# First rows of a Fourier and token-mixing kernel in a hand-made order, with imaginary products woven in and small tiles declared first

## The chip, the cores and the metric

The kernel runs on one core of a Trainium2 chip. Its engines each work through a queue of their own and wait for each other by semaphores: PE (TensorE) multiplies matrices, ACT (ScalarE) and DVE (VectorE) work element by element, POOL (GpSimd) and SP (SyncE) mostly issue transfers. The metric is the device time of one execution in microseconds (us). Before the change it is 887.15 us, the median of three runs from 886.62 to 887.22.

## The reference

`x` has 2048 rows (tokens) of 640 values in float32. Each row is normalized to `xn`. The output is the sum of `x`, a two-dimensional Fourier transform of `xn` of which the real part is kept, and a two-layer network across the token axis.

```python
x = A_x
xn = _layernorm(x, axis=-1)
# _A_ref: a = xn @ dft_hid_re.T, b = xn @ dft_hid_im.T, y = dft_seq_re @ a - dft_seq_im @ b
# _B_ref: u = gelu(xn^T @ w1 + b1), y = (u @ w2 + b2)^T
return x + _A_ref(xn, A_dft_seq_re, A_dft_seq_im, A_dft_hid_re, A_dft_hid_im) + _B_ref(xn, B_w1, B_b1, B_w2, B_b2)
```

## The kernel before, in words

**Precision.** Every float32 operand of a product is split into a high part (`high`, a copy on ACT that rounds to the product's format, L111) and a low part (`low`, a subtraction on DVE, L114). A product of two operands is three matmuls (`three`, L122 to L124): high by high, high by low, low by high. Each loads its own weights: 128 rows by 128 columns of the normalized `x`, while 512 columns of a Fourier matrix move through.

**Steps.** The work is a list of steps. A step cuts one loaded piece of a matrix of 128 x 512 (its *top* is the high part on ACT, its *bottom* the low part on DVE; three places `cut0` to `cut2` are taken in turn) and multiplies it. `turn_of(i)` issues, in this order: the loads planned for turn i, the reads of finished banks, the work on rows, the top of step i + 2, extras, background jobs, the bottom of step i + 2, and the matmuls of step i.

**The first columns.** The first 16 steps (`BLOCK`) work with the first eight groups of 128 rows. Step i has m = i // 8 (real or imaginary Fourier matrix) and k = i % 8 (group of rows), and five products (15 matmuls), one per 128 channels of `x`, each into a PSUM bank of its own. The banks of the real half are read after step 7 (L434), those of the imaginary half after step 15, and both are stored by POOL. Ahead of group k's first product, the group of rows has to be loaded, its mean and variance found (`moments`, DVE, L166 and L167), a square root taken (`root`, DVE L173 and ACT L174), the two factors worked out by four or five small DVE instructions (`inverse` and `offset`, L180 to L189), the rows normalized in place (`normalize`, ACT, L213), and split into high (ACT, two copies of 512 and 128 columns) and low (DVE).

**Order.** Turns up to 7 are issued outside the block with a manual schedule, so a scheduler orders their instructions on each engine. From turn 8 on the order is that of the program. SP issues the loads of rows (L414) and pieces (L415), and waits where a place is still in use; ACT, DVE and PE work strictly through their own queues.

**Warming up.** While the first loads are under way PE multiplies a tile of zeros (`idle`) 20 times (L108).

**Second part.** After the first columns come seven groups of 32 steps each (`columns`), 216 matmuls of 512 columns in a group. They work with sums of rows that background jobs make: the first three groups with those of the lower half of the rows, the last four with those of the upper half. The weights lie in eight operand places `slab0` to `slab7` of 17,920 bytes per partition; place `slab7` serves the last four groups' every fourth row, `n13`. Behind them come three more stages with matmuls of 320 columns.

**Places.** Tiles of the pool `keep` lie one behind another in the order in which their tags are first declared. Before the change that is: `b1_sb`, `b2_sb`, `one`, then `slab7` (by the tile `idle`), then the three small tiles `mv`, `norm` and `again` of 128 bytes per partition each, then `slab4`, `slab5`, `slab0` to `slab3` and the rest.

Of the kernel before, what the change touches and what calls it, by code (L numbers as in the profile page):

```python
# [8 lines left out]
F32 = mybir.dt.float32  # L9
R32 = mybir.dt.float32r  # L10
BF16 = mybir.dt.bfloat16
AF = mybir.ActivationFunctionType
# [28 lines left out]

# [13 lines left out]
def fnet_plus_mixer(  # L55
# [45 lines left out]
    one = keep.tile([P, 1], F32, name="one")  # L101
# [8 lines left out]
    def high(hi, src):  # L110
        nc.scalar.activation(hi, src, AF.Copy)  # L111

    def low(lo, src, hi):
        nc.vector.tensor_sub(lo, src, hi.bitcast(F32))  # L114
# [4 lines left out]
    def three(psum, w, m, first, last):  # L119

        (wh, wl), (mh, ml) = w, m
        nc.tensor.matmul(psum, wh, mh, start=first, stop=False, skip_group_check=True)  # L122
        nc.tensor.matmul(psum, wh, ml, start=False, stop=False, skip_group_check=True)  # L123
        nc.tensor.matmul(psum, wl, mh, start=False, stop=last, skip_group_check=True)  # L124
# [63 lines left out]
    def offset(to, ks):  # L188
        nc.vector.scalar_tensor_tensor(to[:, 1, ks], mv[:, ks, 0], -1.0, to[:, 0, ks], op0=ALU.mult, op1=ALU.mult)  # L189

    def factors(ks):
        inverse(norm[:, 0, ks], *root(mv[:, ks, 1]))
        offset(norm, ks)
# [15 lines left out]

        return [rooted, inverted]  # L210

    def normalize(k, row, by):
        nc.scalar.activation(row, row, AF.Identity, scale=by[:, 0, k : k + 1], bias=by[:, 1, k : k + 1])  # L213


    def pair_at(tag):
# [27 lines left out]
    def fifth(a, which, i):  # L244
        return a[:, which, 7 * Q + i * P : 7 * Q + (i + 1) * P]
# [4 lines left out]
    def sums_of_rows(h, q, row, lower, apart=False):  # L250
# [37 lines left out]
        return [job1, job2, job3, job4] + [job5] * apart + [job6]  # L288


    x_slab = [
        keep.tile([P, 7, D], F32, name="x0", tag="slab4"), keep.tile([P, 1, D], F32, name="x1", tag="slab5"),
    ]
    x_in = [x_slab[k // 7][:, k % 7, :] for k in range(8)]
    for q in range(4):
        place_fixed(0, q)

    def first_rows(k):

        normalize(k, x_in[k], norm)  # L300
# [31 lines left out]
    def later_moments(q):  # L332

        def get():
            for i in range(2):
                nc.sync.dma_start(later_pair(q)[:, i, :], x_rows[8 + q + 4 * i])

        loads[6 + 2 * q].append(get)
        for i in range(2):
            extras[8 + 2 * q + i].append(lambda i=i: moments(8 + q + 4 * i, later_pair(q)[:, i, :]))  # L340

    def later_factors():

# [49 lines left out]
    def c_tile():  # L393

        i = c_turn[0] = (c_turn[0] + 1) % 6
        return c_place[i // 3][:, i % 3, :]

    def store_y(h, m, c, j, t):
        if h == 0:
            nc.gpsimd.dma_start(y_part[m][c][:, j, :], t)  # L400
        else:
            nc.gpsimd.dma_start(y_part[m][c][:, j, :], t, accum_op=ALU.add)

    def first_columns():

        raw = pieces[1].rearrange("p a q c -> p (a q) c")
        banks = {}
        for i in range(BLOCK):
            m, k = i // 8, i % 8

            def load(m=m, k=k, i=i):
                if m == 0:
                    for r in ROWS_AT.get(k, ()):
                        nc.sync.dma_start(x_in[r], x_rows[r])  # L414
                nc.sync.dma_start(raw[:, i % 8, :], dft_seq[m * NC, k])  # L415

            def rows(m=m, k=k):
                if m == 0:
                    first_rows(k)
                    for k0, k1 in GROUPS_AT.get(k, ()):  # L420
                        for r in range(k0, k1):
                            moments(r, x_in[r])
                        factors(slice(k0, k1))

            def products(w, m=m, k=k):
                for j in range(ND):
                    if k == 0:
                        banks[j] = psum[(5 * m + j) % 8]
                    three(banks[j], channels(k, j), w, k == 0, k == 7)

            def read(m=m):
                for j in range(ND):
                    c = c_tile()
                    nc.scalar.activation(c, banks[j], AF.Copy)  # L434
                    store_y(0, m, 0, j, c)

            loads[i - LOADS].append(load)
            sums[i - AHEAD].append(rows)
            steps.append(cut_piece(lambda i=i: raw[:, i % 8, :], CH) + (products,))
            if k == 7:  # L440
                reads[i + 1].append(read)
        loads[-LOADS].append(lambda: None)

    def columns(g, h, c):

# [363 lines left out]
        )  # L809


    first_columns()
    first_sums = [sums_of_rows(0, q, lambda q=q: x_in[q], lambda q=q: x_in[q + 4], True) for q in range(4)]
    for q in range(4):
        later_moments(q)
# [41 lines left out]
    for t in range(NS // 2):  # L857
        down(1, t, ("ca", "cb")[t % 2])

    ready = {}  # L860

    def do_jobs(n, short=False):

        while n > 0 and jobs and not (short and isinstance(jobs[0], tuple)):
# [24 lines left out]
            steps[i][2](ready.pop(i))  # L889


    by_hand = 8
# [58 lines left out]
```

## Time and profile before

| | us |
|---|---|
| time, median of three runs | 887.15 |
| the profiled execution's own time | 887.16 |
| its span, first to last instruction | 884.9 |
| PE busy | 877.2 |
| DVE busy | 701.8 |
| ACT busy | 525.5 |
| POOL busy | 123.2 |

The span is what the profile sees of the program; 2.26 us of the execution lie around it. The profile's page lists busy time by engine and by line; the views used below are the waits (who waited for whom, with the total, the number of times and the longest) and the timeline (start and length of each instruction, with the idle time before it in brackets and what ended it). A matmul's length in the timeline is not its cost: matmuls overlap, and the cost of one is the distance between two starts.

### The profile page before, as it was taken

Reading aid. Unit: us, or ns where it says so; the run is one execution under the profiler, and the core shown is the slowest. Engines: PE = TensorE matmul, PEld = TensorE weight load, DVE = VectorE, ACT = ScalarE, POOL = GpSimd, SP = SyncE. Lnnn points to the kernel's source line nnn. Section 1 sums busy time; section 2 is a strip of 40 time slices with the busy share of each in tenths; the row PEclk is TensorE's granted clock in tenths of the full one; section 3 lists DMA queues with packets and bytes.
Section 4 is the critical chain, followed back from the end, with each engine's and each line's share of the span. In section 5 each row is a group of like instructions: output and inputs, shape, how many; then the busy total and the mean of one; then the engine's idle time right before and its main releaser. Section 6 shows DMA issues by size and latency. Waiting matters only on the chain.

```text
span 884.9 us, 14021 instructions
## 1 busy us (share of the span) xinstructions
PE 877.2 (99%) x4964; PEld 798.8 (90%) x4964; DVE 701.8 (79%) x1181; ACT 525.5 (59%) x953; POOL 123.2 (14%) x166
## 2 busy tenths in 40 slices
PE   8999999999999999999999999999999999999998
PEld 5888888888888888888999999999999999999998
DVE  8577888796787978787877887998678968986776
ACT  6546576664565566557565555675477766655553
POOL 0101000101121111222010101000122211111111
PEclk9999999999999999999999999999999999999999
DMA  8941463719475555869766766553478797756875
GB/s 292 319 144 66 151 253 102 268 48 329 87 206 89 154 136 114 225 83 184 180 124 156 163 142 193 159 180 133 131 170 182 174 253 183 164 129 133 156 173 124
DMA packets 85542, 147.15 MB, mean 166 GB/s; under 512 B 8416, under 2 KB 35296, under 8 KB 85216
## 3 DMA queue, kind: packets, MB, share of 16 engines
q1 hardware_dynamic: 64848, 95.72, 33.3%
q0 software_dynamic: 20624, 50.54, 30.0%
q8 instruction: 39, 0.64, 0.3%
q14 instruction: 31, 0.25, 0.1%
HBM read 99.63 MB, written 51.84 MB: 171 GB/s over the span
## 4 chain that ended last, share of the span: by engine, by line
PE 96%; DVE 2%; ACT 1%; DMA 1%; issue 0%; SPq 0%
PE psum L124 32%; PE psum L123 32%; PE psum L122 32%; DMA pieces<-in_dft_seq 1%; DVE piece L114 0%; DVE st L166 0%; ACT x L213 0%; DVE n L114 0%; DVE shid L114 0%; ACT piece L111 0%; DVE pair L117 0%; DVE pieces L662 0%; DVE pieces L117 0%; SPq L414 0%; ACT shid L111 0%
## 5 line engine op out<-in xcount | busy, mean ns | idle before, releaser
L114 DVE TENSOR_TENSOR piece<-pieces,piece 128x512 fp32r<-128x512 f32 (+2 forms) x506 | 346.6, 688 | 147.7 <-ACT piece L111 144.3
L111 ACT ACTIVATE piece<-pieces 128x512 fp32r<-128x512 f32 (+2 forms) x506 | 317.9, 629 | 235.1 <-PE psum L124 161.0
L122 PE MATMUL psum<-piece,n 128*128 128x512 f32 x584 | 228.4, 391 | 2.5 <-ACT n L111 2.5
L123 PE MATMUL psum<-piece,n 128*128 128x512 f32 x584 | 228.3, 391 | 0.0
L124 PE MATMUL psum<-piece,n 128*128 128x512 f32 x584 | 227.4, 391 | 0.0
L122 PEld LDWEIGHTS psum<-piece,n 128*128 128x128 f32 x584 | 109.6, 188 | 27.2 <-ACT n L111 3.8
L123 PEld LDWEIGHTS psum<-piece,n 128*128 128x128 f32 x584 | 109.7, 188 | 25.6 <-DVE piece L114 2.0
L124 PEld LDWEIGHTS psum<-piece,n 128*128 128x128 f32 x584 | 109.7, 188 | 23.1
L124 PE MATMUL psum<-sup,piece 128*128 128x320 f32 x392 | 121.5, 310 | 0.0
L124 PE MATMUL psum<-sdown,piece 128*128 128x320 f32 x392 | 121.1, 309 | 0.0
L123 PE MATMUL psum<-sdown,piece 128*128 128x320 f32 x392 | 121.0, 309 | 0.0
L123 PE MATMUL psum<-sup,piece 128*128 128x320 f32 x392 | 121.0, 309 | 0.0
L122 PE MATMUL psum<-sup,piece 128*128 128x320 f32 x392 | 121.0, 309 | 0.0
L122 PE MATMUL psum<-sdown,piece 128*128 128x320 f32 x392 | 121.0, 309 | 0.0
L117 DVE TENSOR_TENSOR pieces<-pieces 128x512 f32<-128x512 f32 (+3 forms) x142 | 112.5, 793 | 2.6
L124 PE MATMUL psum<-shid,piece 128*128 128x320 f32 x280 | 86.9, 310 | 0.1
L123 PE MATMUL psum<-shid,piece 128*128 128x320 f32 x280 | 86.5, 309 | 0.0
L122 PE MATMUL psum<-shid,piece 128*128 128x320 f32 x280 | 86.5, 309 | 0.0
L712 ACT ACTIVATE pair<-psum 128x320 f32<-128x320 f32 x104 | 45.3, 436 | 60.1 <-PE psum L124 59.6
L124 PEld LDWEIGHTS psum<-sup,piece 128*128 128x128 f32 x392 | 73.6, 188 | 0.3
L122 PEld LDWEIGHTS psum<-sup,piece 128*128 128x128 f32 x392 | 73.6, 188 | 0.0
L123 PEld LDWEIGHTS psum<-sup,piece 128*128 128x128 f32 x392 | 73.6, 188 | 0.0
(95 smaller groups left out, 1007.8 us busy)
## 6 DMA issues: line engine op xcount, KB each, us to landing
pieces<-in_dft_seq SPq DMA_DIRECT2D x128, 256.0 KB, 5.6
pieces<-in_w SPq DMA_DIRECT2D x88, 256.0 KB, 3.8
y<-c POOLq DMA_DIRECT2D x84, 256.0 KB, 6.0
out<-pair POOLq DMA_DIRECT2D x38, 320.0 KB, 5.2
pieces<-y SPq DMA_DIRECT2D x32, 320.0 KB, 3.7
pieces<-in_w SPq DMA_DIRECT2D x32, 192.0 KB, 3.1
out<-in_x SPq DMA_DIRECT2D x16, 320.0 KB, 5.9
up<-pair POOLq DMA_DIRECT2D x8, 640.0 KB, 3.3
```

Source lines behind the costliest of these rows:

```text
L111: nc.scalar.activation(hi, src, AF.Copy)
L114: nc.vector.tensor_sub(lo, src, hi.bitcast(F32))
L117: nc.vector.tensor_sub(to, a, b)
L122: nc.tensor.matmul(psum, wh, mh, start=first, stop=False, skip_group_check=True)
L123: nc.tensor.matmul(psum, wh, ml, start=False, stop=False, skip_group_check=True)
L124: nc.tensor.matmul(psum, wl, mh, start=False, stop=last, skip_group_check=True)
L712: nc.scalar.activation(c, b, AF.Copy)
```

## The change

It concerns the first columns, and the order of declarations.

- **Woven steps.** There are 18 steps in place of 16. The first two groups of rows are multiplied by the real piece (15 matmuls) and, right behind it, by the imaginary piece for three of the five channel groups (9 matmuls). The two remaining products of these groups in the imaginary half come last, as two steps of 6 matmuls. The number of matmuls and of loaded pieces is the same; two pieces are cut twice.
- **Order within a step.** A step runs all its high by high matmuls first, then all high by low, then all low by high.
- **Order by hand.** The first eight turns are replaced by a list of words, `START`: `x` and `b` load rows and a piece, `T`, `B` and `P` are a step's top, bottom and matmuls, `M` moments, `R` root, `F` factors, `H` the high part of a group of rows, `N` its normalization in place, `L` its low part. The high part is now normalized straight from the loaded rows (with the first group in pieces of 256, 256 and 128 columns), ahead of the normalization in place.
- **First load.** The first group of rows is loaded as two halves, one of which ACT issues as its first instruction.
- **Sums a step later.** The background jobs begin at turn 10 in place of 8, and the last jobs of each group take the order 2, 3, 0, 1. Moments of two of the later rows move into the list.
- **Bank reads.** The real banks are read at turn 10, three of the imaginary ones at turn 16 and two at turn 18.
- **Warming up.** 13 idle matmuls in place of 20.
- **Places.** `mv`, `norm`, `again` are declared right behind `one`, and the tile of the first rows ahead of `idle`: behind the small tiles now come `slab4`, `slab5`, `slab7`, `slab0` and so on.

```diff
-WARM = 20
-ROWS_AT = {0: (0,), 1: (1,), 2: (2, 3), 3: (4, 5), 4: (6, 7)}
-GROUPS_AT = {0: ((1, 2), (2, 4)), 1: ((4, 6),), 3: ((6, 8),)}
-BLOCK = 16
+WARM = 13
+BLOCK = 18
+FIRST = (
+    [(0, 0, 0, 5), (1, 0, 0, 3), (0, 1, 0, 5), (1, 1, 0, 3)] + [(0, k, 0, 5) for k in range(2, 8)]
+    + [(1, k, 0, 5) for k in range(2, 8)] + [(1, 0, 3, 5), (1, 1, 3, 5)]
+)
+FIRST_AT = [0, 6, 1, 7, 2, 3, 4, 5, 0, 1, 2, 3, 4, 5, 0, 1, 6, 7]
+START = """
+    x0 b0 x1 b1 b2 x2 b3 x3 b4 x4 x5 b5 x6 x7 b6 b7
+    T0 M0 R0 F0 H0 B0 N0 M1 R1 T1 L0 F1 H1 B1 P0
+    M2 T2 N1 B2 L1 b8 P1 M3 T3 R2-3 F2-3 H2 B3 P2
+    M4 T4 N2 B4 L2 b9 P3 M5 H3 T5 R4-5 N3 B5 F4-5 L3 b10 e0 P4
+    M6 H4 T6 N4 B6 L4 b11 P5 H5 M7 R6-7 T7 N5 B7 F6-7 L5 b12 e1 P6
+    H6 T8 M8 N6 B8 L6 b13 P7 H7 T9 M12 N7 B9 L7
+"""
...
+    one = keep.tile([P, 1], F32, name="one")
+    mv = keep.tile([P, NS, 2], F32, name="mv")
+    norm = keep.tile([P, 2, NS], F32, name="norm")
+    again = keep.tile([P, 2, NS], F32, name="again")
...
+    x_slab = [
+        keep.tile([P, 7, D], F32, name="x0", tag="slab4"), keep.tile([P, 1, D], F32, name="x1", tag="slab5"),
+    ]
+    x_in = [x_slab[k // 7][:, k % 7, :] for k in range(8)]
+    nc.scalar.dma_start(x_in[0][:, H2:], x_rows[0][:, H2:])
...
-    mv = keep.tile([P, NS, 2], F32, name="mv")
-    norm = keep.tile([P, 2, NS], F32, name="norm")
-    again = keep.tile([P, 2, NS], F32, name="again")
...
-    def normalize(k, row, by):
-        nc.scalar.activation(row, row, AF.Identity, scale=by[:, 0, k : k + 1], bias=by[:, 1, k : k + 1])
+    def normalize(k, row, by, to=None):
+        nc.scalar.activation(
+            row if to is None else to, row, AF.Identity, scale=by[:, 0, k : k + 1], bias=by[:, 1, k : k + 1]
+        )
...
-        high(two(0), src)
-        high(fifth(a, 0, k // 4), x_in[k][:, 2 * Q :])
-        low(two(1), src, two(0))
-        low(fifth(a, 1, k // 4), x_in[k][:, 2 * Q :], fifth(a, 0, k // 4))
+        whole = [(two, src), (lambda which: fifth(a, which, k // 4), x_in[k][:, 2 * Q :])]
+        if which == 0 and k == 0:
+            whole[:1] = [(lambda which, b=b: two(which)[:, b, :], src[:, b, :]) for b in range(2)]
+        for to, t in whole:
+            if which == 0:
+                normalize(k, t, norm, to(0))
+            else:
+                low(to(1), t, to(0))
...
+            for n, (rows, cols) in enumerate(((0, 0), (0, 1), (1, 0))):
+                for j in range(j0, j1):
+                    begin, end = (2, 1) if m == 1 and j >= 3 else (0, 7)
+                    if n == 0 and k == begin:
+                        banks[m, j] = psum[(5 * m + j) % 8]
+                    nc.tensor.matmul(
+                        banks[m, j], channels(k, j)[rows], w[cols], start=n == 0 and k == begin,
+                        stop=n == 2 and k == end, skip_group_check=True,
+                    )
...
+        reads[10].append(lambda: read(0, range(ND)))
+        reads[16].append(lambda: read(1, range(3)))
+        reads[18].append(lambda: read(1, range(3, ND)))
...
-    timed[8].append(lambda: jobs.extend(j for part in (slice(4), slice(4, 6)) for js in first_sums for j in js[part]))
+    timed[10].append(lambda: jobs.extend(
+        [j for js in first_sums for j in js[:4]] + [j for q in (2, 3, 0, 1) for j in first_sums[q][4:]]
+    ))
...
-    for i in range(-LOADS, by_hand):
-        if i == -AHEAD:
-            moments(0, x_in[0])
-            factors(slice(0, 1))
-        turn_of(i, 0)
     with tc.manual_schedule():
-        for i in range(by_hand, len(steps) + 1):
+        for word in START.split():
+            start[word[0]](*map(int, word[1:].split("-")))
+        for i in range(8, len(steps) + 1):
```

More of the change, by code (lines that the diff above doesn't have):

```diff
@@ L94, in fnet_plus_mixer @@
     b2_sb = keep.tile([P, NS], F32, name="b2_sb")
+    one = keep.tile([P, 1], F32, name="one")
+    mv = keep.tile([P, NS, 2], F32, name="mv")
+    norm = keep.tile([P, 2, NS], F32, name="norm")
+    again = keep.tile([P, 2, NS], F32, name="again")
     out_rows = [out[t * P : (t + 1) * P, :] for t in range(NS)]
     x_rows = [x[t * P : (t + 1) * P, :] for t in range(NS)]
+    x_slab = [
[3 more added lines that the diff above has]
+    nc.scalar.dma_start(x_in[0][:, H2:], x_rows[0][:, H2:])
     part_up = [dram.tile([P, 2, D], F32, name=f"up{r}") for r in range(NF2)]
     y_part = [[dram.tile([P, ND, CH], F32, name=f"y{m}{c}") for c in range(NC)] for m in range(2)]
-    one = keep.tile([P, 1], F32, name="one")
     nc.vector.memset(one, 1.0)
@@ L288, in sums_of_rows, with first_rows @@
         return [job1, job2, job3, job4] + [job5] * apart + [job6]
[L291 to L294, printed above, removed]
     for q in range(4):
         place_fixed(0, q)
-    def first_rows(k):
-        normalize(k, x_in[k], norm)
+    def first_rows(k, which):
         a = fixed[0][k % 4]
@@ L330, in later_pair, with later_load, later_moments @@
         return later[0][:, q] if q < 3 else later[1]
[L332 to L338, printed above, removed]
+    def later_load(q):
         for i in range(2):
-            extras[8 + 2 * q + i].append(lambda i=i: moments(8 + q + 4 * i, later_pair(q)[:, i, :]))
+            nc.sync.dma_start(later_pair(q)[:, i, :], x_rows[8 + q + 4 * i])
+    def later_moments(k):
+        moments(k, later_pair(k % 4)[:, (k - 8) // 4, :])
     def later_factors():
@@ L407, in first_columns @@
         banks = {}
[L408 to L441, printed above, removed]
@@ L442, in first_columns, with load, products @@
-        loads[-LOADS].append(lambda: None)
+        vq = {}
+        def load(i):
+            m, k = FIRST[i][:2]
+            nc.sync.dma_start(raw[:, FIRST_AT[i], :], dft_seq[m * NC, k])
+        def products(w, m, k, j0, j1):
+            for n, (rows, cols) in enumerate(((0, 0), (0, 1), (1, 0))):
[7 more added lines that the diff above has]
+                    )
@@ new lines, in read @@
+        def read(m, js):
+            for j in js:
+                c = c_tile()
+                nc.scalar.activation(c, banks[m, j], AF.Copy)
+                store_y(0, m, 0, j, c)
+        for i, (m, k, j0, j1) in enumerate(FIRST):
+            steps.append(
+                cut_piece(lambda i=i: raw[:, FIRST_AT[i], :], CH)
+                + (lambda w, at=(m, k, j0, j1): products(w, *at),)
+            )
+        reads[10].append(lambda: read(0, range(ND)))
+        reads[16].append(lambda: read(1, range(3)))
@@ new lines, in first_columns, with row, top, bottom @@
+        reads[18].append(lambda: read(1, range(3, ND)))
+        for i in range(14, 16):
+            loads[i - 6].append(lambda i=i: load(i))
+        def row(k):
+            if k == 0:
+                nc.sync.dma_start(x_in[0][:, :H2], x_rows[0][:, :H2])
+            else:
+                nc.sync.dma_start(x_in[k], x_rows[k])
+        def top(i):
+            steps[i][0]()
+        def bottom(i):
+            ready[i] = steps[i][1]()
+        def run(i):
+            steps[i][2](ready.pop(i))
@@ new lines, in rooted, with factored @@
+        def rooted(k, to=None):
+            ks = slice(k, (to or k) + 1)
+            vq[k] = root(mv[:, ks, 1])
+        def factored(k, to=None):
+            ks = slice(k, (to or k) + 1)
+            inverse(norm[:, 0, ks], *vq[k])
+            offset(norm, ks)
+        return {
+            "x": row, "b": load, "e": later_load, "T": top, "B": bottom, "P": run,
+            "M": lambda k: moments(k, x_in[k]) if k < 8 else later_moments(k), "R": rooted, "F": factored,
+            "H": lambda k: first_rows(k, 0), "N": lambda k: normalize(k, x_in[k], norm),
+            "L": lambda k: first_rows(k, 1),
+        }
@@ L809, in down @@
         )
-    first_columns()
+    ready = {}
+    start = first_columns()
     first_sums = [sums_of_rows(0, q, lambda q=q: x_in[q], lambda q=q: x_in[q + 4], True) for q in range(4)]
-    for q in range(4):
-        later_moments(q)
-    timed[8].append(lambda: jobs.extend(j for part in (slice(4), slice(4, 6)) for js in first_sums for j in js[part]))
+    for q in range(2, 4):
+        loads[4 + 2 * q].append(lambda q=q: later_load(q))
+    for i, k in enumerate((9, 13, 10, 14, 11, 15)):
+        extras[8 + i].append(lambda k=k: later_moments(k))
+    timed[10].append(lambda: jobs.extend(
+        [j for js in first_sums for j in js[:4]] + [j for q in (2, 3, 0, 1) for j in first_sums[q][4:]]
+    ))
     for g in range(2 * NC - 1):
@@ L858, in fnet_plus_mixer @@
         down(1, t, ("ca", "cb")[t % 2])
-    ready = {}
     def do_jobs(n, short=False):
@@ L889, in turn_of @@
             steps[i][2](ready.pop(i))
-    by_hand = 8
-    for i in range(-LOADS, by_hand):
-        if i == -AHEAD:
-            moments(0, x_in[0])
-            factors(slice(0, 1))
-        turn_of(i, 0)
     with tc.manual_schedule():
-        for i in range(by_hand, len(steps) + 1):
+        for word in START.split():
+            start[word[0]](*map(int, word[1:].split("-")))
+        for i in range(8, len(steps) + 1):
             n_jobs, short = (1, i < BLOCK), False
```

## The prediction

> **What bounds the kernel now.** I read the page first, then PE's waits, then the timeline of the first 30 us on PE, ACT and DVE, then PE's timeline again in the last four groups.
>
> ```profile
> span 884.9 us, 14021 instructions
> PE 877.2 (99%) x4964; PEld 798.8 (90%) x4964; DVE 701.8 (79%) x1181; ACT 525.5 (59%) x953; POOL 123.2 (14%) x166
> ```
>
> PE is the bound. Where does it still stand idle? Its waits over the whole run are two rows:
>
> ```profile
> PE psum L122 <- ACT n L111: 2.5, 3, 1.5
> PE psum L108 <- DVE idle L105: 1.2, 1, 1.2
> ```
>
> All three waits on `n`, the rows' high parts, lie ahead of the first three steps:
>
> ```profile
> 1.23 6.65 PE L108 MATMUL psum<-idle 128*128 128x512 bf16 x20 [1.23 <-DVE idle L105]
> 9.42 0.50 PE L122 MATMUL psum<-piece,n 128*128 128x512 f32 x1 [1.54 <-ACT n L111]
> 13.44 0.50 PE L122 MATMUL psum<-piece,n 128*128 128x512 f32 x1 [0.30 <-ACT n L111]
> 17.80 0.50 PE L122 MATMUL psum<-piece,n 128*128 128x512 f32 x1 [0.65 <-ACT n L111]
> 21.34 0.39 PE L122 MATMUL psum<-piece,n 128*128 128x512 f32 x1
> 24.74 0.39 PE L122 MATMUL psum<-piece,n 128*128 128x512 f32 x1
> ```
>
> From 21.34 on a step of 15 matmuls takes 24.74 - 21.34 = 3.40, so 0.2267 each. By 21.34 there were 45, worth 10.20: the products stand as if they had run without a gap from 11.14. I call this the virtual start. Whatever moves it moves the end, since PE shows no wait afterwards. Why is the first product as late as 9.42?
>
> ```profile
> 4.43 0.63 ACT L111 ACTIVATE piece<-pieces 128x512 fp32r<-128x512 f32 x1 [2.19 <-DMA pieces<-in_dft_seq]
> 5.17 0.20 ACT L174 ACTIVATE q<-v 128x1 f32<-128x1 f32 x1
> 7.19 0.63 ACT L111 ACTIVATE piece<-pieces 128x512 fp32r<-128x512 f32 x1 [1.82 <-DMA pieces<-in_dft_seq]
> 7.73 0.91 ACT L213 ACTIVATE x<-x,norm 128x640 f32<-128x640 f32 x1
> 8.75 0.81 ACT L111 ACTIVATE n<-x 128x512 fp32r<-128x512 f32 x2
> ...
> 5.71 0.15 DVE L180 RECIPROCAL r<-q 128x1 f32<-128x1 f32 x1
> 7.15 0.10 DVE L189 SCALAR_TENSOR_TENSOR norm<-mv,norm 128x1 f32<-128x1 f32 x1
> ```
>
> The root is done at 5.37, but the factors only at 7.25, with the next rows' moments in between on DVE; ACT stands behind a second piece that lands at 7.19, then normalizes 640 columns, then copies.
>
> The last four groups, whose waits are too short for the list, hide a second loss. Starts of steps of nine matmuls, first in an early group, then in a late one:
>
> ```profile
> 71.66 0.39 PE L122 MATMUL psum<-piece,n 128*128 128x512 f32 x1
> 73.70 0.39 PE L122 MATMUL psum<-piece,n 128*128 128x512 f32 x1
> ...
> 217.68 0.39 PE L122 MATMUL psum<-piece,n 128*128 128x512 f32 x1
> 219.72 0.40 PE L122 MATMUL psum<-piece,n 128*128 128x512 f32 x1
> 221.83 0.40 PE L122 MATMUL psum<-piece,n 128*128 128x512 f32 x1
> 223.92 0.39 PE L122 MATMUL psum<-piece,n 128*128 128x512 f32 x1
> ```
>
> 71.66 and 217.68 begin ordinary steps of 2.04. At 219.72 comes the step with weights `n13`: 2.11, and the step behind it 2.09. The same place in the next groups starts at 269.26, 318.76 and 368.29, so a late group takes 49.5, where 216 matmuls at 0.2267 are 48.96.
>
> **The change: the first product.** The real piece stays SP's second load, so ACT's top (4.43 to 5.06) and root (5.17 to 5.37) stay. The ACT-issued half row costs ACT about an SP issue (0.4) before its table load of 1.28, over by 2.5 and idle until 4.43: nothing. The four factor operations (0.15, 0.20, 0.15, 0.12) now follow each other with 0.04 between: 5.42 to 6.2. Then ACT normalizes 256 columns into `n`, a form the trace does not have: not below the plain copy of 256 (0.41), not above the normalization of 640 (0.91). I take 0.59, the copy plus the 0.18 by which a normalization of 640 exceeds a copy of 640 (0.73). First product at 6.25 + 0.59 + 0.05 = 6.9 (6.7 to 7.2), with 13 idle matmuls over at about 6.3.
>
> **What is late next.** A restart costs 0.11 (first distance 0.34 at 9.42) and some 0.05 in the next ten.
> - Step 0's low by high part, ten matmuls on, is due at 9.33. Its `L` waits for `N` (640 columns, ACT, about 7.75 to 8.66), then 0.69: 9.44. Lost 0.1 and a restart, 0.25.
> - Step 1 (nine matmuls) is the cover for rows 1: bottom ready near 10.95, due at 11.4; `H1` near 11.2 and `L1` near 13.8, due at 12.8 and 15.0. Nothing.
> - Step 3's bottom stands on DVE behind M3 (1.1), the root's round trip and five factor operations (1.0): ready 17.0, due 16.85. Lost 0.15 and a restart, 0.3.
> - From step 4 DVE needs per group of rows 1.1 (moments: two of 0.44, one of 0.20) + 0.5 (half of five factor operations) + 0.6 (piece) + 0.9 (low parts of 512 and 128) = 3.1 against 3.40 of PE, and ACT 0.80 + 0.47 + 0.91 + 0.63 = 2.8. Covered; if each were 10% dearer DVE would set the pace.
> - Step 10's fourth product needs bank 0 read. Its last write is five matmuls before step 9's end, the read takes 0.6: done 0.7 ahead of need, bank 1 some 0.4. Without it, at most 0.5.
> - Steps 16 and 17 last 1.36 in place of 3.40: 4.08 less cover. In the old order step 17's low part ended at 63.74 for a matmul near 67.8, a lead of 4.1. Lead used up, three bank reads (0.6 each) stand ahead of step 18's top: 0 to 1.8 lost; I take 0.35, two restarts, since half of the jobs there wait only for each other.
>
> Virtual start: 6.9 + 0.16 (first restart) + 0.25 + 0.3 + 0.35 = 7.95 against 11.14: **3.2 gained**, bounds 1.7 and 4.3.
>
> **Costs taken as nothing.** The new matmul order changes bank and weights every time. In the first steps of before, where banks alternate, distances average 0.2315; but after later short stalls, in the ordinary order, they are 0.231 to 0.236 as well. I take zero; upper bound 240 x 0.0048 = 1.1. Two more pieces (0.63 ACT, 0.69 DVE each) lie in the slack above. SP carries the same 16 pieces, issued earlier; its longest wait for a raw place now is 3.2, and behind it stand only loads due two steps later. Loads take 6.0 to land; row 4, issued near 4.9, is due near 17. POOL stores ten banks still, the last two a step later; their places come round again after six steps (6.0 to landing): covered.
>
> **The change: places.** `slab7` lies at a distance of 17,920 + 384 from the next place, all others at multiples of 512 from each other (17,920 = 35 x 512). With the small tiles first, all eight agree. The late steps ahead of `n13`, with `n10` to `n12`, take 2.04 for nine matmuls, and what follows `n13` is slow only for that step: `n13` is the only slow late weights tile and the only one out of step. If the distance is the cause, four groups lose 49.53 - 48.96 = 0.57 no more: about **2.2 gained**, bounds 0 and 2.3; I take 2.2.
>
> The Trainium skill (TensorE: Matmul & The Clock Gate, Part 2) holds that PE has two independent read ports and that loading the next weights takes no bandwidth from the running matmul. By it no place could matter, and the sum would be 884.0, the time of the first rival below. The trace differs: 2.11 against 2.04 shows that something about this tile matters, though not that it is the distance.
>
> Sum on the profiled execution's own 887.16 (span 884.9 + 2.26), which is the median of the runs but for 0.01: 887.16 - 3.2 - 2.2 = **881.8**.
>
> **The rivals.**
> - *Places change nothing* (0.15). `slab7` was also the lowest place of all; now `slab4` with `n10` is. If low is what is slow, `n10` inherits it. For: low and out of step are the same tile in this trace. Against: in the stages with 320 columns the two tiles in `slab7` move at 0.1469, others at 0.1467, so low alone isn't slow there. 887.16 - 3.2 = 884.0.
> - *The start is eaten up* (0.08). DVE or ACT sets the pace in steps 2 to 9 and 16 to 20, or the matmul order costs its 1.1. For: DVE is 15.67 of the first 20 busy already. Against: half of that is order, not work. Gain 1.0 + 2.2: 884.0; with places idle too, 886.2.
> - *The other side: a cold start* (0.02). The idle matmuls start 0.43 apart until 5.47, then 0.22. With 13, warm speed has to come before the products do. If it came late, each product at 0.43 would lose 0.2; 27 of them cancel 5.4, 36 make the kernel slower by 0.2%, 889. Against: the warm distance came 4.5 after the first idle matmul, and 6.9 is 5.7 after it.
> - *Nothing measurable* (0.03): both gains small, 886.5.
>
> The skill's page on the clock gate (Part 1) says the window is free-running and about 3.4 us. By that the switch could fall as late as 1.23 + 6.8 = 8.0, an estimate; some five products would then be cold and the sum would be 882.8.
>
> **How the numbers follow.** The forecast has 0.72; its own range is 880.7 to 882.9 (start 2.1 to 4.3 gained). The range adds the 884.0 cases, which are nearly all of the rest: 880.8 to 884.3. A difference of 0.2%, or 1.8, is about what a measurement of this kernel can tell from no change. Faster by more than that is below 885.4: 0.72 + 0.15 + 0.06 = 0.93. Within: 0.02 + 0.03 = 0.05. Slower: 0.02.
>
> **What would show it.** First product between 6.7 and 7.2; waits of PE on DVE of a few tenths near 9.4 and 17; a step boundary worth a virtual start near 7.6 before step 16 and 8 after 20. Late groups of 49.0, with the `n13` step at 2.04. I would be wrong through late groups still at 49.5, a wait of PE near step 16 above 1, or distances above 0.23 in all of the first 16 steps.

## The result

The changed kernel takes 881.61 us (median of six runs, 880.92 to 882.16), the kernel before, on the same chip, 887.21 (six runs, 886.62 to 887.49). The ratio is 0.9937, with a 95% interval of 0.9926 to 0.9949: faster by 0.6%. The forecast was 881.8, in a range of 880.8 to 884.3. The profiled execution took 881.44; its page says:

```profile
span 879.6 us, 14010 instructions
PE 873.8 (99%) x4957; PEld 797.8 (91%) x4957; DVE 706.0 (80%) x1183; ACT 529.3 (60%) x956; POOL 123.3 (14%) x166
```

The span fell by 884.94 - 879.57 = 5.37. Starts of matmuls, read off PE's timeline, divide it. The virtual start of a product is its start less 0.2267 for each product ahead of it, as in the prediction; products are counted from 0, and the seven groups begin with product 240.

| | before | after | difference | predicted |
|---|---|---|---|---|
| first product | 9.42 | 6.80 | -2.62 | -2.5 |
| lost behind it, up to product 240 | 1.72 | 0.70 | -1.02 | -1.0 |
| lost in products 240 to 300 | 0 | 0.10 | +0.10 | +0.35 |
| groups 1 to 3, without that | 148.06 | 148.07 | +0.01 | 0 |
| groups 4 to 7 | 198.06 | 195.97 | -2.09 | -2.2 |
| the stages with 320 columns | 469.13 | 469.06 | -0.07 | 0 |
| last matmul to the span's end | 4.15 | 4.48 | +0.33 | 0 |

The last row belongs to this one execution: in a later run of the same kernel it is 4.09. What lies around the span varies in the same way: 1.87 here, 2.22 before (887.16 - 884.94), and between 1.78 and 2.34 in the profiled executions below.

**The start.** PE's timeline (start, length, instruction, count) now shows two rows up to 24 us:

```profile
1.23 5.68 PE L134 MATMUL psum<-idle 128*128 128x512 bf16 x13 [1.23 <-DVE idle L131]
6.80 17.41 PE L441 MATMUL psum<-piece,n 128*128 128x512 f32 x73
```

The waits of `n` that stood at 9.42, 13.44 and 17.80 are gone from this list. Short ones are left, and the waits of PE's weight loads show them (in total, times, longest), from 9 to 12 us and from 12 to 24 us:

```profile
PEld psum L441 <- DVE n L140: 0.4, 1, 0.4
```

```profile
PEld psum L441 <- DVE piece L140: 0.4, 1, 0.4
```

The first is the low part of group 0 in step 0, the second the bottom of step 3. Each moves the virtual start by some 0.25, a wait of about 0.1 and a restart. The chain ahead of the first product, in the timelines of ACT and DVE:

```profile
0.75 0.40 ACTq L123 DMA_DIRECT2D x<-in_x  x1
...
4.54 0.63 ACT L137 ACTIVATE piece<-pieces 128x512 fp32r<-128x512 f32 x1 [1.86 <-DMA pieces<-in_dft_seq]
5.08 0.19 ACT L195 ACTIVATE q<-v 128x1 f32<-128x1 f32 x1
6.15 1.48 ACT L234 ACTIVATE n<-x,norm 128x256 fp32r<-128x256 f32 x3 [0.88 <-DVE norm L210]
```

```profile
4.74 0.15 DVE L194 TENSOR_SCALAR v<-mv 128x1 f32<-128x1 f32 x1
...
5.30 0.17 DVE L201 RECIPROCAL r<-q 128x1 f32<-128x1 f32 x1 [0.40 <-ACT q L195]
...
5.95 0.16 DVE L210 SCALAR_TENSOR_TENSOR norm<-mv,norm 128x1 f32<-128x1 f32 x1
```

The root ends at 5.27, 0.10 earlier than before; the factors follow each other and end at 6.11, 1.14 earlier; from there to the first product it is 0.69 in place of 2.17, since ACT has neither a second piece nor 640 columns ahead of the first 256 (1.48). These two make the 2.62.

**The late groups.** Starts of steps of nine matmuls; the step with `n13` begins at 216.18:

```profile
214.14 0.39 PE L148 MATMUL psum<-piece,n 128*128 128x512 f32 x1
...
216.18 0.39 PE L148 MATMUL psum<-piece,n 128*128 128x512 f32 x1
...
218.22 0.39 PE L148 MATMUL psum<-piece,n 128*128 128x512 f32 x1
...
220.26 0.39 PE L148 MATMUL psum<-piece,n 128*128 128x512 f32 x1
```

All are 2.04 apart, where 2.11 and 2.09 stood before; a late group takes 48.99 in place of 49.52.

### The profile page after: what moved, and what is told of

Same layout as the page of the kernel before. It is cut to its first block, busy times and chain, and to the rows that moved or that the text cites. A ratio compares the mean times of both kernels' runs of the same rounds, so it can differ in the third digit from the quotient of the medians.

```text
span 879.6 us, 14010 instructions
## 1 busy us (share of the span) xinstructions
PE 873.8 (99%) x4957; PEld 797.8 (91%) x4957; DVE 706.0 (80%) x1183; ACT 529.3 (60%) x956; POOL 123.3 (14%) x166
## 4 chain that ended last, share of the span: by engine, by line
PE 98%; DVE 1%; ACT 0%; issue 0%
PE psum L149 30%; PE psum L150 30%; PE psum L148 30%; PE psum L441 6%; PE psum L134 1%; DVE piece L140 0%; DVE shid L140 0%; ACT piece L137 0%; DVE pair L143 0%; DVE pieces L712 0%; DVE pieces L143 0%; ACT shid L137 0%; ACT pair L664 0%; ACT c L561 0%; DVE pair L758 0%
## 5 line engine op out<-in xcount | busy, mean ns | idle before, releaser
L149 PE MATMUL psum<-piece,n 128*128 128x512 f32 x504 | 196.7, 390 | 0.0
L148 PE MATMUL psum<-piece,n 128*128 128x512 f32 x504 | 196.2, 389 | 0.0
L150 PE MATMUL psum<-piece,n 128*128 128x512 f32 x504 | 196.2, 389 | 0.0
L149 PEld LDWEIGHTS psum<-piece,n 128*128 128x128 f32 x504 | 94.6, 188 | 22.1 <-DVE piece L140 2.6
L148 PEld LDWEIGHTS psum<-piece,n 128*128 128x128 f32 x504 | 94.6, 188 | 19.8
L150 PEld LDWEIGHTS psum<-piece,n 128*128 128x128 f32 x504 | 94.6, 188 | 19.3
L150 PEld LDWEIGHTS psum<-sup,piece 128*128 128x128 f32 x392 | 73.6, 188 | 0.3
L148 PEld LDWEIGHTS psum<-sup,piece 128*128 128x128 f32 x392 | 73.6, 188 | 0.0
L149 PEld LDWEIGHTS psum<-sdown,piece 128*128 128x128 f32 x392 | 73.6, 188 | 0.0
```

## The experiments

The theory is the prediction's: an earlier first product whose gain the weaving keeps, and late groups that gain because all operand places now agree modulo 512 bytes. The rivals tested: the low place, the matmul order, the cold start, the half row. "Loss behind the first product" is the virtual start at product 240 less the first product's start. A matmul's distance is the mean from the matmuls of one weights tile to the next start, distances over 250 ns left out. The runs of places share one chip, on which the kernel before takes 887.3; those from the warm-up to the weaving share another, on which it takes 886.71. The changed kernel was not run beside them, so the time of a single run there says little by itself, and what it shows is read from its trace.

### Places

**The places alone**, on the kernel before:

```diff
     one = keep.tile([P, 1], F32, name="one")
+    mv = keep.tile([P, NS, 2], F32, name="mv")
+    norm = keep.tile([P, 2, NS], F32, name="norm")
+    again = keep.tile([P, 2, NS], F32, name="again")
...
-    mv = keep.tile([P, NS, 2], F32, name="mv")
-    norm = keep.tile([P, 2, NS], F32, name="norm")
-    again = keep.tile([P, 2, NS], F32, name="again")
```

> The kernel before with mv, norm and again declared right behind one, nothing else moved: slab7 stays the lowest operand place and comes into step with the others (all at multiples of 512 bytes from each other). Distance theory: the four late groups fall from 49.50 to 49.53 us each to 49.0, steps with n13 take 2.04 for nine matmuls, virtual start stays at 11.1; time 887.2 - 2.1 = 885.1. Low-place theory: groups stay at 49.5, time 887.2.

Measured: 885.48 (884.44 to 885.9) against 887.3; ratio 0.998, interval 0.997 to 0.9989. The start is unchanged (virtual start 11.09), the late groups take 49.03 each, and the distance of `n13` falls from 233.3 to 226.7 ns. `slab7` is still the lowest place here, so being low costs nothing.

**The small tiles back behind three places**, on the changed kernel:

```diff
-    mv = keep.tile([P, NS, 2], F32, name="mv")
-    norm = keep.tile([P, 2, NS], F32, name="norm")
-    again = keep.tile([P, 2, NS], F32, name="again")
...
     idle = keep.tile([P, CH], BF16, name="idle", tag="slab7")
+    mv = keep.tile([P, NS, 2], F32, name="mv")
+    norm = keep.tile([P, 2, NS], F32, name="norm")
+    again = keep.tile([P, 2, NS], F32, name="again")
```

> The changed kernel with the three small tiles behind slab4, slab5 and slab7: these three are out of step by 128 bytes, slab6 and the early places are not. Distance theory: n10, n11 and n13 are all slow (about 0.233 a matmul), n12 is not by itself; late groups between 49.5 and 50.3, time 882.5 to 887. Low-place theory: n10 alone is slow, in the lowest place; groups 49.5, time 883.7.

Measured in one run: 884.89. `slab4`, `slab5` and `slab7` are now out of step with the rest by 128 modulo 256; the late groups take 50.04, and `n10`, `n11` and `n13` move at 232.4 to 232.8 ns. Three slow tiles cost about twice what one cost, not three times: the group lost 1.05 over the 48.99, against 0.53. These three are in step with each other, which settles one question. In each late group `n13`, `n10`, `n11`, `n10` and `n11` follow each other in five steps, 36 matmuls in all. The two steps of nine among them, with `n10` and then `n11`, from PE's timeline:

```profile
240.53 0.39 PE L148 MATMUL psum<-piece,n 128*128 128x512 f32 x1
...
242.62 0.40 PE L148 MATMUL psum<-piece,n 128*128 128x512 f32 x1
...
244.72 0.40 PE L148 MATMUL psum<-piece,n 128*128 128x512 f32 x1
```

Both take 2.09 to 2.10, and the 36 last 8.36 (from 239.14 to 247.50), or 232.3 ns each, though only the first of them has weights out of step with those ahead. So it is not the distance from one weights tile to the next that counts.

**Other distances**, on the changed kernel: gaps of 64 bytes ahead of `slab4` and `slab5`, 128 ahead of `slab7` and 256 behind it, which put `slab4` 64, `slab5` 128 and `slab7` 256 out of step with the rest.

```diff
+    def gap(n, name):
+        keep.tile([P, n // 4], F32, name=name)
+    gap(64, "gap4")
...
+    gap(64, "gap5")
...
+    gap(128, "gap7")
...
+    gap(256, "gap0")
```

> The changed kernel with unused tiles between the places: slab4 (n10) out of step by 64 bytes, slab5 (n11) by 128, slab7 (n13) by 256, slab6 (n12) by none. Distance theory: n11 is slow as n13 was before (0.233); n10 and n13 tell which distances count, without a forecast of mine for 64 and 256; n12 at 0.2267 except right behind a slow one. Low-place theory: n10 alone slow.

Measured in one run: 883.27, late groups of 49.70. `n10` (64 bytes out) moves at 233.3 ns, `n11` (128) at 232.8, `n13` (256) at 226.6. PE's timeline, starts of the steps with `n10`, `n11`, `n12`, `n13` and the next:

```profile
209.77 0.40 PE L154 MATMUL psum<-piece,n 128*128 128x512 f32 x1
...
211.87 0.39 PE L154 MATMUL psum<-piece,n 128*128 128x512 f32 x1
...
213.96 0.40 PE L154 MATMUL psum<-piece,n 128*128 128x512 f32 x1
...
216.03 0.39 PE L154 MATMUL psum<-piece,n 128*128 128x512 f32 x1
...
218.07 0.40 PE L154 MATMUL psum<-piece,n 128*128 128x512 f32 x1
```

2.10 with `n10`, 2.09 with `n11`, 2.07 with `n12`, which follows a slow one, and 2.04 with `n13`. A distance of 256 is harmless; the prediction's 512 was finer than needed.

**The highest place out of step**, on the changed kernel, 128 bytes ahead of `slab6`:

```diff
+            if q == 2:
+                keep.tile([P, 32], F32, name="gap6")
```

> The changed kernel with 128 unused bytes ahead of slab6, the highest place: n12 alone is out of step by 128 bytes. Distance theory: n12 takes about 0.233 a matmul, the late groups about 49.5, time 881.6 + 2.1 = 883.7. Low-place theory: nothing changes, 881.6, groups 49.0.

Measured in one run: 883.24, late groups of 49.52, as in the kernel before. The slow tile is now `n12` (233.3 ns), with `n13` behind it at 229.4. Steps with `n11`, `n12`, `n13` and the next:

```profile
211.79 0.39 PE L148 MATMUL psum<-piece,n 128*128 128x512 f32 x1
...
213.84 0.40 PE L148 MATMUL psum<-piece,n 128*128 128x512 f32 x1
...
215.94 0.40 PE L148 MATMUL psum<-piece,n 128*128 128x512 f32 x1
...
218.03 0.39 PE L148 MATMUL psum<-piece,n 128*128 128x512 f32 x1
```

2.05, 2.10, 2.09: the pair that stood at `n13` has moved with the distance. The rival "low place" falls.

It is open whether what counts is the distance to the moving pieces or the weights' own address modulo 256: in every run, the places in step with the moving pieces are also those with the same address modulo 256. The kernel was never tried with all places and moving pieces shifted together.

### The warm-up

```diff
-WARM = 13
+WARM = 20
```

> The changed kernel with 20 idle matmuls in place of 13. They ended at 7.88 before (their last start 7.50, 0.216 apart), and the first product is ready at 6.80. My theory: products start near 7.72, lows are all ready by then, so the two waits in steps 0 and 3 go and the virtual start is about 7.9 in place of 7.5; time 882.0. Rival (the idle matmuls do not stand in the way): 881.6.

Measured in one run: 881.24. The first product's start stands 28 ns behind that of the last idle matmul, at 7.32, and the next start 0.42 behind it. Yet the virtual start is 7.54, against 7.49 and 7.32 in two executions of the changed kernel: what the products start later, they no longer wait in steps 0 and 3 (loss behind the first product 0.21). The expected 0.4 did not come, for another reason too: here the idle matmuls went from 427 to 216 ns apart at 5.3, in the changed kernel's run not until all 13 were over.

```diff
-WARM = 13
+WARM = 6
```

> The changed kernel with 6 idle matmuls: they end near 4.0 and PE stands idle until 6.8. Cold-start theory: the clock is still held back or is held back again, the first products start 0.43 apart for up to 4 us, 5 to 20 of them, and the virtual start is 1 to 4 later; time 882.6 to 885.6. Rival (warming up is not needed for a start at 6.8): distances of 0.23 from the first product, 881.6.

Measured in one run: 882.15. The first product is at 6.82 as before; eight products stand 427 ns apart, and the loss behind the first product is 1.77 in place of 0.7. A table of stretches (time, then PE busy, weight loads, DVE, ACT, POOL, then the granted clock, then the DMA share and GB/s):

```profile
4.48:7.89 3.41, 1.07 (x5) 0.78 (x6) 2.84 (x12) 2.42 (x6) 0.00 (x0) 1.00 0.98 349
7.89:11.30 3.41, 3.41 (x10) 2.63 (x9) 2.64 (x10) 2.33 (x5) 0.00 (x0) 0.50 1.04 407
```

The products start warm at 6.82 and go cold at 7.89, for 3.41. Eight cold products at 0.2 each are 1.6, of which 0.5 replaces the waits in steps 0 and 3; the price is the remaining 1.1, far from enough to change the sign. The virtual start moved by the expected 1 to 4; the time lies below the expected 882.6 to 885.6.

### The order within a step

```diff
-            for n, (rows, cols) in enumerate(((0, 0), (0, 1), (1, 0))):
-                for j in range(j0, j1):
+            for j in range(j0, j1):
+                for n, (rows, cols) in enumerate(((0, 0), (0, 1), (1, 0))):
```

> The changed kernel with the matmuls of a step in the old order, three for one bank and then the next. My theory (the new order costs nothing by itself and moves the need for the low parts back): distances of 0.2267 in both orders from step 4 on; in step 0 the third matmul now needs L0 (9.36 in place of the 11th), so about 1.8 is lost there and some of it is cover for later; virtual start 8.7 to 9.3, time 882.8 to 883.4. Rival (alternating banks is dearer): distances above 0.23 in steps 4 to 15 of the changed kernel and 0.2267 here, and up to 1.1 comes back.

Measured in one run: 884.01, a virtual start of 10.38. The third matmul needs the low part of the rows, so PE waits at once:

```profile
6.80 0.73 PE L441 MATMUL psum<-piece,n 128*128 128x512 f32 x2 [0.52 <-ACT n L234]
9.36 3.68 PE L441 MATMUL psum<-piece,n 128*128 128x512 f32 x9 [1.83 <-DVE n L140]
```

That is the expected wait. Not expected was that the clock then fell:

```profile
5.45:8.86 3.41, 1.56 (x6) 0.49 (x4) 2.57 (x10) 2.68 (x6) 0.00 (x0) 1.00 1.03 384
8.86:12.27 3.41, 2.91 (x7) 2.33 (x8) 3.14 (x11) 2.34 (x5) 0.00 (x0) 0.50 1.05 407
```

One product's distance is 592 ns, five are 427 and one is 325; against 338 for a warm restart and 227 that is 0.25 + 5 x 0.2 + 0.1 = 1.35, about what the virtual start exceeds the expected one by. Once steady, the distance is 226.7 ns in this order as in the other: changing bank and weights with every matmul costs nothing, and the order is worth what it hides.

### The weaving

16 plain steps in place of 18, with the half row, the factors in a row, the direct normalization, the order within a step and the places kept; the bank reads go back to turns 8 and 16 and the background jobs to turn 8:

```diff
-FIRST = (
-    [(0, 0, 0, 5), (1, 0, 0, 3), (0, 1, 0, 5), (1, 1, 0, 3)] + [(0, k, 0, 5) for k in range(2, 8)]
-    + [(1, k, 0, 5) for k in range(2, 8)] + [(1, 0, 3, 5), (1, 1, 3, 5)]
-)
+FIRST = [(m, k, 0, 5) for m in range(2) for k in range(8)]
...
-    M2 T2 N1 B2 L1 b8 P1 M3 T3 R2-3 F2-3 H2 B3 P2
+    M2 R2 N1 F2 T2 L1 H2 b8 B2 P1
+    M3 R3 N2 F3 T3 L2 b9 H3 B3 P2
...
-        reads[10].append(lambda: read(0, range(ND)))
+        reads[8].append(lambda: read(0, range(ND)))
```

> The changed kernel with 16 plain steps (no imaginary products woven in) and a list of words fitted to them; places, first load, direct high parts, order within a step and idle matmuls as in the changed kernel. First product at 6.8 as there. My theory (the nine extra matmuls on rows 0 and 1 are the cover that DVE needs for rows 1 to 3): DVE needs 3.4 to 3.9 a step, PE waits 0.4 to 0.6 in most of the first seven steps, virtual start 10 to 11; time 884 to 885. Rival (the direct high parts and the order by hand are enough): virtual start below 8, time 882.

Measured: 883.96 (883.83 to 884.09) against 886.71; ratio 0.9968, interval 0.9957 to 0.998. The first product is at 6.64, but each of the first seven steps waits for its rows' low part. Waits of the weight loads from 9 to 36 us:

```profile
PEld psum L441 <- DVE n L140: 3.6, 7, 0.7
PEld psum L441 <- ACT n L234: 0.8, 1, 0.8
```

The loss behind the first product is 3.65, the virtual start 10.28. So of the 2.8 by which the first product is earlier than in the kernel before, 0.9 reaches the end; with the weaving it is 3.6 to 3.8, more than the 2.8, since the old waits in the steps behind go too. The weaving is the cover without which the early start is given back. The order of words is one of many for plain steps, and a better one might lose less.

### What is left in the start, and the half row

The next runs share one chip; the changed kernel ran beside them again.

> The changed kernel beside the next three, as their yardstick: 881.3 to 881.9, virtual start 7.5, late groups 48.99, the end 0.3 later behind the last matmul than in the kernel before if that lag belongs to the kernel, and not if it was that one execution's.

Measured: 881.31 (881.17 to 881.83) against 886.98; ratio 0.9938. Virtual start 7.32, first product 6.64, loss behind it 0.68, late groups 49.03, the end 4.09 behind the last matmul.

**Step 3's bottom ahead of the factors:**

```diff
-    M2 T2 N1 B2 L1 b8 P1 M3 T3 R2-3 F2-3 H2 B3 P2
-    M4 T4 N2 B4 L2 b9 P3 M5 H3 T5 R4-5 N3 B5 F4-5 L3 b10 e0 P4
+    M2 T2 N1 B2 L1 b8 P1 M3 T3 R2-3 B3 T4 F2-3 H2 P2
+    M4 N2 B4 L2 b9 P3 M5 H3 T5 R4-5 N3 B5 F4-5 L3 b10 e0 P4
```

> The words of the hand-made order change in one place: step 3's bottom stands ahead of the factors of rows 2 and 3, and row 3's high part behind them. Theory (PE waits 0.24 at step 3 because its bottom stands behind five factor operations on DVE): that wait goes, the virtual start moves from 7.49 to about 7.25, the time by the same 0.2 (881.3 or so), unless row 3's rows come 0.6 later and PE waits for them a step later. Rival (the wait is row 3's or the piece's landing): no change of the virtual start, 881.6.

Measured: 881.19 (880.82 to 881.44). In the changed kernel the bottom stood behind the factors, at 16.11, here it stands in the root's round trip (DVE's timelines):

```profile
16.04 0.16 DVE L210 SCALAR_TENSOR_TENSOR norm<-mv,norm 128x2 f32<-128x2 f32 x1
16.11 0.69 DVE L140 TENSOR_TENSOR piece<-pieces,piece 128x512 fp32r<-128x512 f32 x1
```

```profile
14.90 0.17 DVE L194 TENSOR_SCALAR v<-mv 128x2 f32<-128x2 f32 x1
14.98 0.69 DVE L140 TENSOR_TENSOR piece<-pieces,piece 128x512 fp32r<-128x512 f32 x1
15.59 0.16 DVE L201 RECIPROCAL r<-q 128x2 f32<-128x2 f32 x1
```

The wait at step 3 is gone, and the loss behind the first product falls from 0.68 to 0.47. The first product was late in this execution (6.90; 6.57 to 6.80 in five others with the same opening: the changed kernel twice and three of the places' runs), so the virtual start is 7.37, and the times don't tell the two kernels apart.

**That, and two more of DVE's orders:**

```diff
+                if k == 0 and n == 2:
+                    normalize(0, x_in[0][:, : 2 * Q], norm)
...
+            order = [(n, j) for n in range(3) for j in range(j0, j1)]
+            if m == k == 0:
+                order = [(n, j) for n in range(2) for j in range(4)] + [(0, 4), (1, 4)] + [(2, j) for j in range(5)]
...
-                extras[s0 + at[e]].append(lambda names=names, e=e: sub(*(b(n, 2 * e, 2) for n in names)))
+                (late if at[e] in (6, 8) else extras)[s0 + at[e]].append(lambda names=names, e=e: sub(*(b(n, 2 * e, 2) for n in names)))
```

> The one before, and two more: in step 0 the last 128 columns' low product needs nothing but the first group's parts (their products are put last and ACT normalizes the first group's 512 columns in place ahead of the last 128), so that the low parts of the first group come 0.3 earlier; and in the groups of 32 steps two subtractions on DVE stand behind the piece's bottom of the same turn in place of ahead of it. Theory (the wait of 0.26 in step 0, that of 0.24 in step 3 and the short stalls at step 10 of the early groups are all DVE's order, not its work): virtual start 7.0 to 7.1 in place of 7.49, early groups 49.1 in place of 49.4, 880.5 to 881.0. Rival (DVE is full there, what is moved ahead of one thing is late for the next): virtual start 7.3 to 7.6, early groups as they were, 881.4 to 881.9.

Measured: 881.11 (880.58 to 881.57), ratio 0.9935 (0.9922 to 0.9947): the lowest median, but not told apart from the changed kernel's 0.9938. In the start the theory holds: no wait is left, the loss is 0.33, all of it at the first matmul, and the virtual start is 7.05. In the groups of 32 steps it falls: groups 1 to 3 take 148.09 together as before. The short stall at step 10 of a group is still there (the start at 78.19 comes 360 ns behind the one ahead), and the timelines of DVE and ACT say why:

```profile
77.45 0.69 DVE L140 TENSOR_TENSOR piece<-pieces,piece 128x512 fp32r<-128x512 f32 x1 [1.45 <-ACT piece L137]
```

```profile
75.17 1.72 ACT L234 ACTIVATE later<-later,norm 128x640 f32<-128x640 f32 x2
76.80 1.87 ACT L137 ACTIVATE piece<-pieces 128x512 fp32r<-128x512 f32 x3
```

DVE is free 1.45 ahead of the bottom and waits for the top, which ACT cuts behind two normalizations of 640 columns. It is ACT's order that would have to change there; that was not tried.

**The first row whole:**

```diff
-    nc.scalar.dma_start(x_in[0][:, H2:], x_rows[0][:, H2:])
...
-            if k == 0:
-                nc.sync.dma_start(x_in[0][:, :H2], x_rows[0][:, :H2])
-            else:
-                nc.sync.dma_start(x_in[k], x_rows[k])
+            nc.sync.dma_start(x_in[k], x_rows[k])
```

> The changed kernel with row 0 loaded whole by SP, as the kernel before loads it, in place of one half by SP and one by ACT. This tells what of the earlier first product (9.42 to 6.80) is the half row's and what is the order of the factors. Theory (the order is nearly all of it): the moments start at 3.82 as before in place of 3.58, the first product 0.25 later at 7.05, the virtual start 7.7, 881.9. Rival (the two halves land far earlier than the whole, and more of the start hangs on them): the first product at 7.4 or later, 882.2 or more.

Measured in two runs: 881.45 (881.17 to 881.72), first product 6.86, loss behind it 0.66. That is 0.22 later than in the changed kernel's run beside it (6.64), near the expected 0.25, but only 0.06 later than in its first one (6.80). ACT's timeline with the row whole, then that of the changed kernel's run beside it:

```profile
4.40 0.63 ACT L136 ACTIVATE piece<-pieces 128x512 fp32r<-128x512 f32 x1 [2.16 <-DMA pieces<-in_dft_seq]
5.12 0.20 ACT L194 ACTIVATE q<-v 128x1 f32<-128x1 f32 x1
```

```profile
4.34 0.63 ACT L137 ACTIVATE piece<-pieces 128x512 fp32r<-128x512 f32 x1 [1.66 <-DMA pieces<-in_dft_seq]
4.91 0.20 ACT L195 ACTIVATE q<-v 128x1 f32<-128x1 f32 x1
```

With the row whole the moments end some 0.2 later than with halves, and the root starts at 5.12. With halves it stands behind ACT's top of the first piece: it starts at 4.91 where the top starts at 4.34, and at 5.08 where the top starts at 4.54, as in the first run; there the half row's gain is hidden. So of the 2.6 the half row makes 0.06 to 0.22 in these executions, and the times don't show it; the order of the factors and of ACT makes the rest.

## Why the prediction was right

- *First product 6.9 (6.7 to 7.2).* Right: 6.80, and 6.57 to 6.90 over those six executions, three of them below 6.7. The unseen normalization of 256 columns, taken as 0.59 between 0.41 and 0.91, measured 0.60.
- *First restart 0.16, step 0 0.25, step 3 0.3.* Right: 0.17, 0.25 and 0.25, at the places named, each a real wait of about 0.1 and a restart of 0.11. The reordering of step 3 shows that its cause was the one named.
- *Step 10 nothing, steps 2 to 9 covered by a small slack on DVE.* Right, but for step 3's wait: the virtual start moves by 0.02 from product 15 to product 39, and stands still from product 63 to product 240.
- *"Lead used up, three bank reads stand ahead of step 18's top: I take 0.35."* This is the term that was mis-sized: 0.10 in the profiled execution, 0.03 in the second one, and no distance there is above 245 ns, so the two restarts reckoned in it did not come. With 0.1 of the first product and 0.05 of step 3 it makes the virtual start 7.59 in place of 7.95, a gain of 3.55 in place of 3.2.
- *The new matmul order costs zero, bounds to 1.1.* Right, by the steady 226.7 ns of both orders.
- *Places, 2.2.* Right in mechanism, 0.1 too much: 2.09 here, and 1.94 with the places alone (198.06 less four times 49.03). The premise that alignment goes by 512 was too narrow. And the argument against the low place, taken from the stages with 320 columns, carries less than was thought: there the places hold the moving operand, and the weights are a cut piece. The run with the places alone decides it.
- *The sum* missed by 0.4 on the profiled execution (881.8 against 881.44), 0.2 on the median. The terms' errors are 0.35 too little at the start and 0.1 too much in the places. The rest, +0.33 behind the last matmul and -0.36 around the span, varies from one execution to the next, and that the two cancel is luck. The lower end of the stated range, 880.8, also lies above the forecast's own 880.7, which nothing in the working explains.

Of the rivals, *places change nothing* was excluded by the measured distances: 64 or 128 bytes more in a weights tile's address cost 6 to 7 ns of 227. Behind it stood the Trainium skill's sentence (TensorE: Matmul & The Clock Gate, Part 2) on two independent read ports, so that loading the next weights takes no bandwidth from the running matmul. Taken to mean that no place matters, it differs from these runs; whether bandwidth is what is lost, no run shows. *The start is eaten up* is what the kernel without weaving does. *A cold start* has the price given, 0.2 for each cold product, but was not near: six idle matmuls in place of 13 made eight of them cold, and 36 were needed.

## What to carry to other kernels

Where PE is the bound and shows no waits later on, reckon every early stall in starts of matmuls, as a virtual start: here it moved the end by about as much, and each stall costs a restart of 0.11 besides. An earlier first product is worth only as much as the work that can stand between it and the next operand; give the first operands more products before moving them forward. Compare the steady distances tile by tile, since a loss of 3% in one weights tile of four shows in no list of waits, and look at the tile's address first.

## What the runs showed of the hardware

- **Places.** fp32r weights of 128 x 128 with 512 moving columns start 226.7 ns apart. With the weights tile 64, 128 or 384 bytes (per partition) out of step with the other tiles it is 232.4 to 233.3, with 256 or 512 it is 226.6 to 226.7. The step behind a slow one starts slowly too (2.09 for nine matmuls): its distances run 235, 234, 236, 224 and 231, much as behind a restart. In the stages with 320 columns the places hold the moving operand. There the one that was out of step in the kernel before moved at 146.9 ns, the others at 146.7, and since the distances behind it are shorter, nothing is lost. That speaks for the weights' address rather than the distance, but at another number of columns, so it is not shown.
- **The clock.** With six idle matmuls and with the other order it fell and rose 3.41 us later: 7.89 and 11.30, 8.86 and 12.27 (the stretches shown above read 1.00 and 0.50). In the stretch of 3.41 ahead of each fall PE was busy 1.07 and 1.56. In the run with the first row whole the idle matmuls quickened at 4.59, and no fall came 3.41 later, with PE busy 2.39 in between:

```profile
4.59:8.00 3.41, 2.39 (x11) 1.25 (x10) 2.90 (x12) 2.40 (x6) 0.00 (x0) 1.00 0.99 356
```

  The Trainium skill (TensorE: Matmul & The Clock Gate, Part 1) has a free-running window of 3.4 us and a fall after an idle one. The length agrees; the runs show that a window busy for 46% is idle enough, and one busy for 70% is not, nor one busy for 64% (2.20 from 5.68 to 9.09, in the kernel before).
- **The warm-up's end.** The first idle matmul starts at 1.23 in all runs. The earliest fast distance came at 4.6; in four executions none of the thirteen had come, the last idle matmul starting at 6.33. In two of these (the highest place out of step, and DVE's orders) the first product still had a distance of 483 and 536 ns in place of 338. Thirteen idle matmuls are just enough, not ample.
- **The granted clock at the start.** It reads 1.00 from 1 to 4 us although the idle matmuls stand 427 ns apart there: there the distances tell the clock, and this column doesn't.
